# Attention, an MLP and eight experts in one kernel: the token scatters of the last batches spread out, and five slots' loads made independent of the last batch's scatters

## The chip, the cores and the metric

One core of a Trainium2 chip runs the whole program. The metric is device time in microseconds (us) of one execution; lower is better. The core has the engines that the profile calls PE (matrix multiplication), PEld (loading of its stationary operand), DVE (VectorE), ACT (ScalarE), POOL (GpSimd) and SP (SyncE, which here only issues transfers), and 16 DMA engines that all transfers share.

## The reference, cut to what matters

```python
scores = x @ state.T / sqrt(D); xread = softmax(scores) @ state      # 8 batches, 8 heads, 512 rows, D 64
sread  = softmax(state @ x.T / sqrt(D)) @ x                           # 32 rows of state for each batch
x = concatenate([xread, sread])                                       # 4096 + 512 rows -> 4608 tokens of 512
h = x @ w_in                                                          # 512 -> 2048
x = (h * clip(h + 3, 0, 6) / 6) @ w_out                               # 2048 -> 512
e_idx = argmax(x @ w_gate); gate_w = softmax(x @ w_gate)[e_idx]       # 8 experts, one for each token
eom = 1 / (1 + exp(-(x @ w_output_gate)))
for e in range(8):
    out[mask_e] = gate_w * eom[:, e] * (relu(x[mask_e] @ w1[e]) @ w2[e])   # 512 -> 1024 -> 512
```

## The kernel before

Tokens come in eight batches of 512 rows (the xread part, batches 0 to 7) and a last batch of 256 (the sread part). Each goes through attention and the MLP on PE, 16 steps of the hidden dimension ("ft") a batch; the sread steps are matmuls of line 473 into `h` and of lines 498 to 500 into `o`. While PE works on the next batch, the batch behind it is **routed**, in steps spread over the ft loop: its rows go out to memory (`xd`, line 543) and come back by token (`xt`, line 641), the expert is chosen, and VectorE works out each token's place (`place`, tile `ldsti`). Then POOL issues two kinds of indirect transfer, one for 128 tokens each: `sort_rows` (line 649) scatters rows of 2 KB into `xs`, which is sorted by expert, and `scatter` (line 663) scatters 8 bytes a token, its number and its weight, into the table `tab`. `zero_tails` (line 953) scatters four blocks of zeros into `xs`, from a tile that line 945 fills. Which of the two comes first on POOL is set by the program.

After the last batch, VectorE makes lists of the blocks to work on: `lists1` for blocks that surely hold tokens of batches 0 to 7 (kind "1"), `lists2` for those that depend on the last batch (kinds "m" and "p"). They land in `regs`, `regsm` and `regsu`, and SP reads addresses out of them (TENSOR_LOAD, lines 876 to 895; they can stand in front of SP's other work, and SP works strictly in its order).

The expert phase works through 16 slots of 256 rows, and in between pairs of two blocks of 64 rows. A slot is 8 ft steps: `gemm1` (12 matmuls of line 997, 128x256, into `h`) and `gemm2e` (6 matmuls of lines 1015, 1018 and 1019, 128x512, into `o`) with the pieces `wh`, `wl` (line 993), `vh`, `vl` (lines 1002, 1003), `hh` (line 1006) and `hl` (line 1007) that ACT and DVE make. At ft 3 of slot s, `turn` transposes the rows of slot s+1 on DVE (line 917) and rounds them (line 938), and `fetch_rows` has SP load the rows of slot s+3 (`xg`, line 897) with their token numbers and weights (`own`, line 906). At the end of a slot `fetch_weights` loads those of the slot after next (line 884, 8 transfers of 512 KB, left out at run time where the expert stays the same). `finish` scales the result by the weight (line 1032) and scatters it to `out` (line 1035). In `gemm1` this says that the low part of ft 6 comes behind the next rows on DVE:

```python
if ft == 6:
    tc.add_manual_dep(i.ins, last_turned[0].name, LATER, reason="the next rows first")
```

Every load of `xg` waits for the row scatters in the list `put`, every load of `own` for the token scatters in `placed`; each scatter waits for those of the batch before. The tiles for the rows, the zeros and the result `y` share a ring of two buffers ("xr"). Where nothing is stated, the order on an engine comes from a scheduler, not from the text alone.

Of the kernel before, what the change touches and what calls it, by code (L numbers as in the profile page):

```python
# [79 lines left out]
def tile_kernel(  # L80
# [421 lines left out]

    placed, put = [], []

# [139 lines left out]
    def sort_rows(r, t0, t1, behind=()):  # L644

        if t0 == 0:
            r.sorted = []
        for t in range(t0, t1):
            i = G.indirect_dma_start(xs, bass.IndirectOffsetOnAxis(ap=r.dsti[:, t:t + 1], axis=0), r.rows[t], None).ins  # L649
            for d in behind:  # L650
                tc.add_manual_dep(i, d.name, DEP, reason="in its time")
            for o in r.sorted:
                tc.declare_no_dep(i, o, reason="places are distinct")
            after(i, put)
            r.sorted.append(i)
        if t1 == r.nt:
            put[:] = r.sorted

    def scatter(r, behind=()):

        new = []
        for t in range(r.nt):
            i = G.indirect_dma_start(tab, bass.IndirectOffsetOnAxis(ap=r.dsti[:, t:t + 1], axis=0),
                                     toku[:, r.tile0 + t, :], None).ins
            for d in behind:
                tc.add_manual_dep(i, d.name, DEP, reason="rows are written first")
            tc.add_manual_dep(i, put[-1].name, LATER, reason="rows are wanted first")
            for o in new:
# [5 lines left out]
    def route(r):  # L674
# [15 lines left out]
        sort_rows(r, 0, r.nt)  # L690
        scatter(r)
        if r.n == 256:
            zero_tails()
        yield
# [192 lines left out]

    def load_rows(bases, n, own_by=None):
# [3 lines left out]
        own = cp.tile([128, 2, 2], U32, tag="own", name="own", bufs=5)  # L892
        a = n // 32
        for j, reg in enumerate(bases):
            base = D.value_load(reg, min_val=0, max_val=NTAB - n)
            for g in range(4):
                i = D.dma_start(xg[32 * g:32 * g + 32, a * j:a * j + a, :],
                                xs[bass.ds(base, n), 128 * g:128 * g + 128].rearrange("(a u) c -> u a c", u=32)).ins
                after(i, put)
            if n == 64:  # L900
                E = own_by or D
                if own_by:
                    base = E.value_load(reg, min_val=0, max_val=NTAB - n)
                i = E.dma_start(own[64 * j:64 * j + 64, 0, :], tab[bass.ds(base, n), :]).ins
# [3 lines left out]
        return own, xg  # L908

# [31 lines left out]

    def zero_tails():

        z = mp.tile([128, DM], F32, tag="xr", name="zeros", bufs=2)
        G.memset(z, 0.0)
        pair = carry.rearrange("p (j two) -> p two j", two=2)
        ends, tails = one("ends", NE // 2), one("tails", NE // 2, U32)
        V.tensor_tensor(ends, pair[:, 1, :], pair[:, 0, :], op=ALU.subtract)
        V.scalar_tensor_tensor(ends, ends, C("half"), pair[:, 0, :], op0=ALU.mult, op1=ALU.add)
        V.tensor_scalar(tails, ends, C("part64"), None, op0=ALU.add)  # L950
        new = []
        for j in range(NE // 2):
            i = G.indirect_dma_start(xs, bass.IndirectOffsetOnAxis(ap=tails[:, j:j + 1], axis=0), z, None).ins
            for o in new:
# [281 lines left out]

    got, turned, lists = {}, {}, {}

    def fetch_rows(s):
        k, j = ORDER[s]  # L1240
        regs = lists[k]
        n = regs.shape[1] // 3 * 2
        if k == "p":
            got[s] = load_rows([regs[0:1, n + u:n + u + 1] for u in (2 * j, 2 * j + 1)], 64, G if s >= first else None)
        else:
            got[s] = load_rows([regs[0:1, n + j:n + j + 1]], 256)

# [17 lines left out]
    for ft in range(16):  # L1265
        held.append((NB, ft, *act(h_sread(ft), 256, False)))
        second(LAG)
        step(later)
        step(later)
        if ft == 5:  # L1270
            while later:
                step(later)
            lists["1"] = lists1()
            fetch_weights(0)
            fetch_rows(0)

            for t in ws[1][0] + ws[1][1]:
                G.tensor_copy(t[0:1, 0, 0:1], got[0][1][0:1, 0, 0:1])
            fetch_weights(1)
# [5 lines left out]
    qa["p"].tile([128, 8], F32, name="gap2")  # L1285
    turned[0] = turn(got[0][1], 2)
    qa["p"].tile([128, 32], F32, name="gap3")
# [5 lines left out]
    def drain(n):  # L1293
        while len(pend) > n:
            s, py, args = pend.pop(0)
            gemm2e(py, *args)
            if args[0] == 7:
                ids, _ = got.pop(s)
                turned.pop(s)
                finish(py, ids, out[0:NX, :] if ORDER[s][0] == "1" else out, s + 1 == first)  # L1300

# [6 lines left out]
    def turn_next(s):  # L1308
        if s + 1 < first:
            turned[s + 1] = turn(got[s + 1][1], 1 if ORDER[s + 1][0] == 'p' else 2)  # L1310
        if s + 3 < first:
            fetch_rows(s + 3)

    def slot(s):
        g = big.index(s)
        for ft in range(8):
            if ft == 0 and s not in turned:
                turned[s] = turn(got[s][1], 1 if ORDER[s][0] == 'p' else 2)
            xh, xl = turned[s]
# [17 lines left out]
    def pair(s):  # L1337
        j = ORDER[s][1]
        if s not in turned:
            turned[s] = turn(got[s][1], 1 if ORDER[s][0] == 'p' else 2)  # L1340
        x, _ = turned.pop(s)
# [11 lines left out]
        for ft in range(8):  # L1353
# [4 lines left out]
            pair2(py, ft, hT[ft // 4])  # L1358
        finish([py], got.pop(s)[0], out)
        if j + 1 < NP and j + 1 != CUT:  # L1360
# [56 lines left out]
```

## Time and profile before

| | us |
|---|---|
| time, median of 3 runs | 1128.01 (1126.42 to 1130.27) |
| time of the profiled execution | 1126.77 |
| its span on the core | 1125.1 |
| PE busy in it | 1079.5 (96%) |
| DVE, ACT, POOL busy | 717.6, 553.3, 114.0 |

Times in the rows are counted from the start of the span. The span lies inside the execution's own time, and the two differ by 1.67 us here. Attention and the MLP of batches 0 to 7 end shortly after 630 us, the sread steps run to 693 us, the expert phase from 694 us to 1108.7 us.

### The profile page before, as it was taken

To read this page: it belongs to the slowest core of one execution; us is meant where nothing else is said; L and a number is where in the kernel's file an instruction comes from. 1 tells how busy PE (TensorE), PEld (TensorE's weight loads), DVE (VectorE), ACT (ScalarE), POOL (GpSimd) and SP (SyncE) were. 2 spreads that over 40 slices of the span, in tenths; PEclk is the share of its full clock that TensorE was granted. 3 is DMA by queue.
4 is the path that set the end of the run, shared out by engine and by line. 5 is a ranking of instruction groups with operands and counts; after the bars stand their busy time and mean duration, and the time that the engine had idled before them with its cause. 6 is when DMAs were issued, how large, how long until landed. Compare 5 with 4: busy or idle time off the path is not lost. (4 is left out here: it accounts for less than half of the span.)

```text
span 1125.1 us, 18656 instructions
## 1 busy us (share of the span) xinstructions
PE 1079.5 (96%) x6764; PEld 850.8 (76%) x6764; DVE 717.6 (64%) x1533; ACT 553.3 (49%) x1058; POOL 114.0 (10%) x122
## 2 busy tenths in 40 slices
PE   4899999999999999999999999999999999999994
PEld 2567777777777777777777889878869877889981
DVE  6997767755746747557455466886556756676640
ACT  4779744433434434334343435556445645665640
POOL 0000001120030020200300220310010110100010
PEclk9999999999999999999999999999999999999997
DMA  6647042622214114220130189267585689921300
GB/s 229 206 133 263 29 134 74 174 75 57 94 40 112 41 38 113 78 58 19 38 75 7 43 215 257 80 202 258 174 314 171 223 265 315 327 57 60 139 19 31
DMA packets 83428, 147.39 MB, mean 131 GB/s; under 512 B 13232, under 2 KB 49840, under 8 KB 83312
## 3 DMA queue, kind: packets, MB, share of 16 engines
q1 hardware_dynamic: 76400, 126.94, 36.8%
q0 software_dynamic: 6928, 19.18, 4.6%
q8 instruction: 55, 0.90, 0.3%
q14 instruction: 45, 0.37, 0.1%
HBM read 146.05 MB, written 29.68 MB: 156 GB/s over the span
## 5 line engine op out<-in xcount | busy, mean ns | idle before, releaser
L498 PE MATMUL o<-gh,wo 128*128 128x512 f32 x512 | 199.2, 393 | 1.7 <-ACT wo L752 1.7
L499 PE MATMUL o<-gh,wo 128*128 128x512 f32 x512 | 200.2, 391 | 0.6 <-DVE wo L753 0.6
L500 PE MATMUL o<-gl,wo 128*128 128x512 f32 x512 | 199.9, 390 | 0.0
L489 DVE SCALAR_TENSOR_TENSOR g<-r,h 128x512 f32<-128x512 f32 x128 | 87.4, 683 | 118.6 <-ACT r L488 118.0
L488 ACT ACTIVATE r<-h 128x512 f32<-128x512 f32 x128 | 76.7, 599 | 164.5 <-PE h L459 164.4
L1003 DVE TENSOR_TENSOR vl<-w2s,vh 128x512 fp32r<-128x512 f32 x128 | 87.7, 689 | 66.9 <-ACT vh L1002 62.9
L1002 ACT CAST vh<-w2s 128x512 fp32r<-128x512 f32 x128 | 78.8, 621 | 81.8 <-PE o L1019 73.5
L490 ACT CAST gh<-g 128x512 fp32r<-128x512 f32 x128 | 79.3, 620 | 80.2 <-DVE g L489 79.3
L491 DVE TENSOR_TENSOR gl<-g,gh 128x512 fp32r<-128x512 f32 x128 | 88.3, 690 | 45.5 <-ACT gh L490 37.9
L498 PEld LDWEIGHTS o<-gh,wo 128*128 128x128 f32 x512 | 95.9, 188 | 27.8 <-issue 4.4
L499 PEld LDWEIGHTS o<-gh,wo 128*128 128x128 f32 x512 | 96.3, 188 | 23.5 <-issue 2.1
L500 PEld LDWEIGHTS o<-gl,wo 128*128 128x128 f32 x512 | 96.1, 188 | 20.4
L993 DVE TENSOR_TENSOR wl<-w1s,wh 128x512 fp32r<-128x512 f32 x128 | 86.9, 687 | 37.3 <-ACT wh L993 29.5
L459 PE MATMUL h<-ah,sh 128*128 128x512 f32 x256 | 106.5, 417 | 4.0 <-ACT sh L446 2.3
L459 PE MATMUL h<-al,sh 128*128 128x512 f32 x256 | 102.3, 400 | 0.3 <-DVE al L290 0.3
L1019 PE MATMUL o<-vh,hl 128*128 128x512 f32 x256 | 100.7, 394 | 1.6 <-DVE hl L1007 1.6
L459 PE MATMUL h<-ah,sl 128*128 128x512 f32 x256 | 100.8, 394 | 0.0
L1018 PE MATMUL o<-vl,hh 128*128 128x512 f32 x256 | 100.3, 392 | 0.0
L649 POOL DMA_INDIRECT xs<-xt,ldsti x34 | 36.1, 1061 | 574.0 <-DVE ldsti L634 525.5
L993 ACT CAST wh<-w1s 128x512 fp32r<-128x512 f32 x128 | 77.9, 621 | 31.7 <-PE h L997 24.6
L997 PEld LDWEIGHTS h<-xh,wh 128*128 128x128 f32 x512 | 76.6, 188 | 15.0 <-DVE hl L1007 2.4
L997 PE MATMUL h<-xh,wh 128*128 128x256 f32 x512 | 82.3, 282 | 1.8 <-DVE hl L1007 1.8
(230 smaller groups left out, 1804.2 us busy)
## 6 DMA issues: line engine op xcount, KB each, us to landing
w1s<-w SPq DMA_DIRECT2D x88, 512.0 KB
w2s<-w SPq DMA_DIRECT2D x88, 512.0 KB
xd<-xr SPq DMA_DIRECT2D x68, 128.0 KB
xt<-xd SPq DMA_DIRECT2D x17, 512.0 KB
xT<-xT SPq DMA_DIRECT2D x16, 512.0 KB
wi<-w_in SPq DMA_DIRECT2D x16, 512.0 KB
wraw<-w_out SPq DMA_DIRECT2D x16, 512.0 KB
xq<-xq SPq DMA_DIRECT2D x16, 512.0 KB
```

The source lines that it names most:

```text
L459: T.matmul(ps, w[:, o:o + 128], a[:, e, :], start=(n == 0), stop=(n == 5))
L489: V.scalar_tensor_tensor(g6, r, 6.0, ps, op0=ALU.min, op1=ALU.mult)
L490: S.copy(gh, g6)
L491: V.tensor_tensor(gl, g6, gh.bitcast(F32), op=ALU.subtract)
L498: T.matmul(po[k][:, :n], woh[ft][:, s], gh, start=first, stop=False)
L499: T.matmul(po[k][:, :n], wol[ft][:, s], gh, start=False, stop=False)
L500: T.matmul(po[k][:, :n], woh[ft][:, s], gl, start=False, stop=last)
L993: last_w[:] = [S.copy(wh, a).ins, V.tensor_tensor(wl, a, wh.bitcast(F32), op=ALU.subtract).ins]
L997: T.matmul(ps, w[:, k, :], x[:, k, :], start=(m == 0), stop=(m == 11))
L1003: V.tensor_tensor(vl, c, vh.bitcast(F32), op=ALU.subtract)
L1018: T.matmul(py[t], hh[:, sl], vl, start=False, stop=False)
L1019: T.matmul(py[t], hl[:, sl], vh, start=False, stop=(ft == 7))
```

## The change

- The token scatter of batch 7 (4 transfers), so far right behind its row scatters, moves to ft 9 of the sread loop.
- The last batch's two token scatters come ahead of its row scatters on POOL, and its four scatters of zeros go out in two halves, some steps later. The memset of the zeros moves from POOL to VectorE.
- The last batch's row, token and zero scatters are declared independent of the loads of the slots of kind "1" (slots 0 to 4): those wait for batch 7's scatters only.
- `own` is loaded when the slot's rows are turned (`turn_rows`), no longer with the rows; the order for the `lists2` step at slot 1 no longer drains the routing steps first.

```diff
@@ -651,6 +659,8 @@
             for o in r.sorted:
                 tc.declare_no_dep(i, o, reason="places are distinct")
+            if r.n == 256:
+                apart(i, later_rows, sooner)
             after(i, put)
@@ -664,7 +674,8 @@
                 tc.add_manual_dep(i, d.name, DEP, reason="rows are written first")
-            tc.add_manual_dep(i, put[-1].name, LATER, reason="rows are wanted first")
+            if r.n == 256:
+                apart(i, later_rows, sooner)
@@ -688,9 +699,16 @@
         sort_rows(r, 0, r.nt)
-        scatter(r)
-        if r.n == 256:
-            zero_tails()
+        if r.n > 256:
+            return
+        yield
+        yield
+        scatter(r, last_w[:1])
+        yield
+        yield
+        zero_tails(0, 2)
+        yield
+        zero_tails(2, 4)
         yield
@@ -897,15 +914,23 @@
                 after(i, put)
+                if put is first_put:
+                    apart(i, sooner, later_rows)
+        return xg
...
+            if placed is first_placed:
+                apart(i, sooner, later_rows)
+        return own
@@ -939,18 +964,23 @@
-        G.memset(z, 0.0)
...
+            V.memset(zeros["z"], 0.0)
...
+        for j in range(j0, j1):
+            i = G.indirect_dma_start(xs, bass.IndirectOffsetOnAxis(ap=zeros["at"][:, j:j + 1], axis=0), zeros["z"], None).ins
+            tc.add_manual_dep(i, last_w[0].name, DEP, reason="in its time")
@@ -1265,17 +1300,23 @@
+        if ft == 9:
+            scatter(unplaced, marks[-1:])
+            first_placed[:] = placed
         if ft == 5:
             while later:
                 step(later)
+            first_put[:] = put
             lists["1"] = lists1()
@@ -1307,15 +1347,13 @@
     def turn_next(s):
         if s + 1 < first:
-            turned[s + 1] = turn(got[s + 1][1], 1 if ORDER[s + 1][0] == 'p' else 2)
+            turn_rows(s + 1)
@@ -1325,8 +1363,6 @@
             if s == 1 and ft == 0:
-                while later:
-                    step(later)
                 lists.update(lists2())
```

Where instructions stand now, at the places that the prediction speaks of:

On POOL, from batch 7's token scatters (`tab<-toku`) to the first results (`out<-y`); the 8 copies stand behind the loading of slot 0. Before:

```order
L663 DMA tab<-toku,ldsti 36096x2 x4
...
L945 MEMSET zeros 128x512
L649 DMA xs<-xt,ldsti 36096x512 x2
L663 DMA tab<-toku,ldsti 36096x2 x2
L953 DMA xs<-zeros,tails 36096x512 x4
L1035 DMA out<-y,own 4096x512 x10
```

Now:

```order
L673 DMA tab<-toku,ldsti 36096x2 x2
L657 DMA xs<-xt,ldsti 36096x512 x2
L981 DMA xs<-zeros,tails 36096x512 x2
L1065 DMA out<-y,own 4096x512 x2
L981 DMA xs<-zeros,tails 36096x512 x2
```

The memset is gone from POOL, the last batch's token scatters stand ahead of its row scatters, and slot 0's two result scatters stand between the two halves of the zeros. Batch 7's four token scatters keep their place in the row of POOL's work; what they wait for has changed.

On SP, from the last batch's rows to the weights of slot 2. Before, the rows and the `own` of slot 3 stand behind 25 reads of registers (TENSOR_LOAD), of which the last five are of lists that `lists2` makes:

```order
L641 DMA xt<-xd 128x2x512
...
L895 TENSOR_LOAD regsm
L895 ISA x2
L876 TENSOR_LOAD regsu
...
L895 TENSOR_LOAD regsu
L895 ISA x2
L897 ISA
L897 DMA xg<-xs 32x8x128
...
L906 DMA own<-tab 128x2x2
L884 ISA
L884 DMA w1s_5999<-w 128x1024
```

Now:

```order
L649 DMA xt<-xd 128x2x512
L914 ISA
L914 DMA xg<-xs 32x8x128
...
L894 TENSOR_LOAD regs_6345
L894 ISA x2
L897 TENSOR_LOAD regs_6345
L897 ISA x2
L902 ISA
L902 DMA w1s_5999<-w 128x1024
```

The reads of `regsm` and `regsu` have left this place, so that the rows of slot 3 and the weights of slot 2 stand in front of everything that waits for `lists2`.

On PE, from slot 1 into slot 2 (`o_7690` and `o_7691` before, `o_7713` and `o_7714` now, are slot 2's sums). Before:

```order
L997 MATMUL h<-xh,wh 128x256 x4
L997 MATMUL h<-xl,wh 128x256 x4
L997 MATMUL h<-xh,wl 128x256 x4
L997 MATMUL h<-xh,wh 128x256 x4
L997 MATMUL h<-xl,wh 128x256 x3
L1015 MATMUL o_7690<-vh,hh 128x512
L1015 MATMUL o_7691<-vh,hh 128x512
L997 MATMUL h<-xl,wh 128x256
L997 MATMUL h<-xh,wl 128x256 x3
```

Now:

```order
L1027 MATMUL h<-xh,wh 128x256 x4
L1027 MATMUL h<-xl,wh 128x256 x4
L1027 MATMUL h<-xh,wl 128x256 x4
L1045 MATMUL o_7713<-vh,hh 128x512
L1045 MATMUL o_7714<-vh,hh 128x512
L1048 MATMUL o_7713<-vl,hh 128x512
L1049 MATMUL o_7713<-vh,hl 128x512
L1048 MATMUL o_7714<-vl,hh 128x512
L1049 MATMUL o_7714<-vh,hl 128x512
```

Before, nearly four steps' first products (43 matmuls) stand ahead of slot 2's first second product; now the two kinds alternate step by step there. The bunched order stands before at the entries of slots 2, 3 and 11 with 43 matmuls, and of slot 7 with 55; now at those of slots 3, 7 and 11, with 43 each. The number of PE's instructions is the same.

## Rows read from the trace of the kernel before

**Rows 1.** The page, part 1: busy time of each engine.

```profile
PE 1079.5 (96%) x6764; PEld 850.8 (76%) x6764; DVE 717.6 (64%) x1533; ACT 553.3 (49%) x1058; POOL 114.0 (10%) x122
```

**Rows 2.** Waits of PE: what it waited for, us in total, times, longest.

```profile
PE h L473 <- issue: 2.4, 5, 0.9
```

**Rows 3.** Timeline of PE in the sread steps: start, us, instruction.

```profile
659.24 0.64 PE L473 MATMUL h<-x1h,wih 128*128 128x256 f32 x4
...
662.09 0.63 PE L473 MATMUL h<-x1h,wih 128*128 128x256 f32 x3
...
669.97 0.67 PE L473 MATMUL h<-x1h,wih 128*128 128x256 f32 x4
```

**Rows 4.** Windows: busy PE, PEld, DVE, ACT, POOL; granted clock, DMA share, GB/s.

```profile
665.00:670.00 5.00, 4.06 (x19) 3.70 (x19) 2.03 (x4) 2.11 (x5) 0.35 (x1) 0.66 0.98 211
670.00:675.00 5.00, 5.00 (x44) 5.00 (x44) 2.61 (x7) 2.62 (x6) 0.00 (x0) 0.99 0.98 255
735.00:740.00 5.00, 3.76 (x22) 2.83 (x20) 5.00 (x17) 2.30 (x5) 0.00 (x0) 1.00 0.17 58
```

**Rows 5.** Timeline of POOL: start, us, instruction, idle before it.

```profile
660.43 1.13 POOL L663 DMA_INDIRECT tab<-toku,ldsti  x1 [0.30 <-issue]
...
732.07 0.96 POOL L1035 DMA_INDIRECT out<-y,own  x1 [12.14 <-ACT y L1032]
```

**Rows 6.** DMA issues, 660:670, median us to landing.

```profile
tab<-toku,ldsti POOLq DMA_INDIRECT x4, 10.2
```

**Rows 7.** DMA issues, 620:640, median us to landing.

```profile
tab<-toku,ldsti POOLq DMA_INDIRECT x4, 3.7
```

**Rows 8.** Timeline of SP's queue: issues of weights, skipped ones too.

```profile
661.55 2.53 SPq L884 DMA_DIRECT2D w1s<-w  x4
...
741.69 1.39 SPq L884 DMA_DIRECT2D w1s<-w  x4
...
781.20 2.49 SPq L884 DMA_DIRECT2D w1s<-w  x4
```

**Rows 9.** Waits of SP's queue.

```profile
SPq L895 <- DVE regsm L803: 13.3, 1, 13.3
```

**Rows 10.** Timeline of DVE: the turn of slot 1's rows, and the end of slot 1.

```profile
710.25 1.42 DVE L917 STREAM_TRANSPOSE xt<-xg 128x256 f32<-128x256 f32 x4
...
739.91 0.75 DVE L1007 SCALAR_TENSOR_TENSOR hl<-h,hh 128x256 fp32r<-128x256 f32 x2
```

**Rows 11.** Timeline of ACT at the entry of slot 2.

```profile
741.79 0.62 ACT L993 CAST wh<-w1s 128x512 fp32r<-128x512 f32 x1 [2.40 <-DMA w1s<-w]
742.32 1.26 ACT L1032 ACTIVATE y<-o,own 128x512 f32<-128x512 f32 x2
```

**Rows 12.** Timeline of PE: end of slot 1, and a regular step of slot 2.

```profile
740.39 0.72 PE L1019 MATMUL o<-vh,hl 128*128 128x512 f32 x2 [1.63 <-DVE hl L1007]
...
753.75 0.63 PE L997 MATMUL h<-xh,wh 128*128 128x256 f32 x4
...
755.15 0.63 PE L1015 MATMUL o<-vh,hh 128*128 128x512 f32 x2
...
756.53 0.63 PE L997 MATMUL h<-xh,wh 128*128 128x256 f32 x4
```

**Rows 13.** Timeline of PE: entries of slots 3, 4 and 7.

```profile
766.25 0.63 PE L997 MATMUL h<-xh,wh 128*128 128x256 f32 x4
...
777.41 0.63 PE L997 MATMUL h<-xh,wh 128*128 128x256 f32 x4
...
793.40 0.74 PE L1015 MATMUL o<-vh,hh 128*128 128x512 f32 x2 [0.49 <-ACT hh L1006]
...
873.68 0.52 PE L997 MATMUL h<-xh,wh 128*128 128x256 f32 x3
...
886.74 0.63 PE L997 MATMUL h<-xh,wh 128*128 128x256 f32 x4
```

**Rows 14.** Tile trow, the other memset of this shape on DVE: ns, start.

```profile
L1069 DVE MEMSET trow<- x1: 485/485/485, 84.4 to 84.4; 128x512 f32 x1
```

More of the change, by code (lines that the diff above doesn't have):

```diff
@@ L500, in gemm2, with apart @@
             T.matmul(po[k][:, :n], woh[ft][:, s], gl, start=False, stop=last)
-    placed, put = [], []
+    placed, put, first_placed, first_put = [], [], [], []
+    sooner, later_rows = [], []
+    def apart(i, mine, others):
+        for o in others:
+            tc.declare_no_dep(i, o, reason="rows of earlier batches")
+        mine.append(i)
     def after(i, others):
@@ L886, in tile_kernel, with load_rows @@
     qa = {}
-    def load_rows(bases, n, own_by=None):
+    def load_rows(bases, n, put):
         xg = qa["p"].tile([128, 8, 128], F32, tag="xg", name="xg", bufs=2) if qa else \
             mp.tile([128, 8, 128], F32, tag="xr", name="xg0", bufs=2)
-        own = cp.tile([128, 2, 2], U32, tag="own", name="own", bufs=5)
         a = n // 32
@@ L899, in load_rows, with load_own @@
                 after(i, put)
+                if put is first_put:
+                    apart(i, sooner, later_rows)
+        return xg
+    def load_own(bases, n, placed):
+        own = cp.tile([128, 2, 2], U32, tag="own", name="own", bufs=5)
+        for j, reg in enumerate(bases):
+            base = D.value_load(reg, min_val=0, max_val=NTAB - n)
             if n == 64:
[L901 to L904, printed above, removed]
+                i = D.dma_start(own[64 * j:64 * j + 64, 0, :], tab[bass.ds(base, n), :]).ins
             else:
@@ L940, in turn, with zero_tails @@
         return xh, xl
-    def zero_tails():
-        z = mp.tile([128, DM], F32, tag="xr", name="zeros", bufs=2)
-        G.memset(z, 0.0)
[L946 to L950, printed above, removed]
+    zeros = {}
+    def zero_tails(j0, j1):
+        if j0 == 0:
+            zeros["z"] = mp.tile([128, DM], F32, tag="xr", name="zeros", bufs=2)
+            V.memset(zeros["z"], 0.0)
+            pair = carry.rearrange("p (j two) -> p two j", two=2)
+            ends, zeros["at"] = one("ends", NE // 2), one("tails", NE // 2, U32)
+            V.tensor_tensor(ends, pair[:, 1, :], pair[:, 0, :], op=ALU.subtract)
+            V.scalar_tensor_tensor(ends, ends, C("half"), pair[:, 0, :], op0=ALU.mult, op1=ALU.add)
+            V.tensor_scalar(zeros["at"], ends, C("part64"), None, op0=ALU.add)
         new = []
-        for j in range(NE // 2):
-            i = G.indirect_dma_start(xs, bass.IndirectOffsetOnAxis(ap=tails[:, j:j + 1], axis=0), z, None).ins
+        for j in range(j0, j1):
+            i = G.indirect_dma_start(xs, bass.IndirectOffsetOnAxis(ap=zeros["at"][:, j:j + 1], axis=0), zeros["z"], None).ins
+            tc.add_manual_dep(i, last_w[0].name, DEP, reason="in its time")
+            apart(i, later_rows, sooner)
             for o in new:
@@ L1242, in fetch_rows, with turn_rows @@
         n = regs.shape[1] // 3 * 2
[L1243 to L1246, printed above, removed]
+        at = (2 * j, 2 * j + 1) if k == "p" else (j,)
+        return [regs[0:1, n + u:n + u + 1] for u in at], 64 if k == "p" else 256
+    def fetch_rows(s):
+        got[s] = load_rows(*place_of(s), first_put if ORDER[s][0] == "1" else put)
+    def turn_rows(s):
+        turned[s] = turn(got.pop(s), 1 if ORDER[s][0] == 'p' else 2)
+        owns[s] = load_own(*place_of(s), first_placed if ORDER[s][0] == "1" else placed)
     big = [s for s, (k, _) in enumerate(ORDER) if k != "p"]
@@ L1267, in tile_kernel @@
         second(LAG)
+        if later and isinstance(later[0], Route):
+            unplaced = later[0]
         step(later)
         step(later)
+        if ft == 9:
+            scatter(unplaced, marks[-1:])
+            first_placed[:] = placed
         if ft == 5:
```

18 lines of the change are left out of this document (7 added, 11 removed).

## The prediction, made before the changed kernel had run

> **What bounds the kernel now.** I read the page first: PE is busy for 1079.5 of the 1125.1 us of the span [rows 1], so all that another engine does counts only where PE stands still for it, and 45.6 us is the most that any order of work could give back. Some 22 us of it are in the first 75 us and 16.4 us behind the last matmul (span 1125.1, last matmul at 1108.7); the change touches neither. Then I read the waits of PE and its timeline between 650 and 900 us, where the moved instructions stand. Three places show time lost.
>
> The first is a pause in the sread steps. Step 7 takes 662.09 − 659.24 = 2.85 us, and step 8 takes 669.97 − 662.09 = 7.88 us with the same matmuls [rows 3]: 5.0 us are lost. PE's waits put 2.4 us of it down to "issue", in 5 pieces [rows 2], that is to no semaphore which the profile shows; the rest is matmuls at a granted clock of 0.66 in the mean over 665 to 670 us [rows 4], part of it at the lower level of 1.2 GHz, after PE had stood still. Two things begin just then: POOL issues batch 7's four token scatters from 660.43 on [rows 5], and SP the 4 MB of slot 0's weights at 661.55 [rows 8]. The DMA engines are then 98% busy, and stay so from 670 to 675 us, when PE is busy for all 5.00 us [rows 4]. So full DMA engines alone do not stop PE; the token scatters among them, or the start of the loads, may.
>
> The second is the entry of slot 2. DVE is busy for all of 735 to 740 us, with `lists2` and the next rows, and PE waits 1.63 us for `hl` [rows 4, 12]. SP has meanwhile stood for 13.3 us before a register of `regsm` [rows 9], so that the (skipped) weight transfers of slot 2 come at 741.69 only [rows 8], and ACT's first piece of them after a wait of 2.40 us [rows 11].
>
> The third is small: the bunched order at the entries of some slots, and 0.49 us before slot 4 [rows 13].
>
> **The change, step by step.** All terms are in the profiled execution's time.
>
> *The memset on DVE.* The same shape took 485 ns on DVE [rows 14]. At its new place, among the `lists2` work, DVE has no gap before the `hl` that PE waits for at 740.39 [rows 10, 12]. It costs 0 if it falls before DVE fills up, and 0.5 if not. The order puts it in the middle of the filled stretch, so I take **+0.4**.
>
> *The bunched order at slot 2 goes.* A regular step is 12 first products, 755.15 − 753.75 = 1.40 us, and 6 second ones, 756.53 − 755.15 = 1.38 us [rows 12]. From 740.39 to 753.75 PE had 48 of the first and 26 of the second kind to do: 4 × 1.40 + 26 × 0.23 = 11.58 us of work. It took 13.36, so 1.78 us were lost behind the late weights and the bunching. Now SP has slot 2's weights in front of all that waits for `lists2`, and PE's order is regular there. The bounds are 0 (another wait is there) and −1.78. I take **−1.7**, because the wait of ACT that fed it, 2.40 us, ended on the weights alone.
>
> *The same at slot 7.* There the bunch shrinks from 55 to 43. The old one took 886.74 − 873.68 = 13.06 us for 60 and 24, which is 5 × 1.40 + 4 × 1.38 = 12.52 us of work: 0.54 lost. One of 43, at slot 3, took 777.41 − 766.25 = 11.16 us for 48 and 18, 9.74 us of work: 1.42 lost [rows 13]. The new bunch has the size of the second row, so I take 1.42 − 0.54 = **+0.9**; the bounds are 0 and +0.9. Slots 3 and 11 keep theirs.
>
> *SP runs earlier.* Slot 4's weights were issued at 781.20 [rows 8], late since SP was late from 741 on, and PE waited 0.49 for the `hh` made of them [rows 13]. SP gains several us before that, so this goes: **−0.5**, with bounds 0 and −0.5.
>
> *`own` with the turn.* Same number of transfers, one slot later. `own` is wanted only when the slot's result is scaled, a slot (8 × 2.78 = 22 us) after its turn; SP's load of it waits for batch 7's token scatters, which land by 672 + 4 × 1.3 + 10.2, about 687 us, before slot 0 begins at 694: 0.
>
> *The last batch's scatters.* Slot 3's first load now stands in front of the reading of the last batch's rows on SP. It waits for the buffer that the turn at 710.25 to 711.67 frees [rows 10]. So those rows are scattered some 8 us later, and the two halves of the zeros go out at about 728 and, behind slot 0's results on POOL (732.07 [rows 5] and one more), at 735 to 737. Landing takes 3.7 us where the DMA engines are quiet [rows 7], so the zeros' tile comes free at about 740. The second result tile takes its buffer, and ACT writes it at 742.32 [rows 11]. The cover is 2 us. It costs 0, and if it were gone, ACT would stand for as long as the zeros are late, with slot 2's pieces of weights behind it, and PE a step later.
>
> *Batch 7's token scatter to ft 9.* This is the large one. It waits for a mark of ft 9 now: about 672 us if the pause stays where it is, 667 if not. SP's loads of the weights of slots 0 and 1 (8 MB) run until about 700 us, so the scatter still falls into full DMA engines. The bounds: −5.0 (the pause needs the scatters and the start of the loads together, and the two are parted now), 0 (it moves with the scatters, or stays with the loads) and +5.0 (both make one). The row nearest to the scatter's new place is that of 10.2 us to land among loads, against 3.7 without [rows 6, 7]; the new place has the loads of the old one, which is why I take **0**. Against it stands that PE ran freely at 670 to 675 us while the same transfers were still landing [rows 4]: it is their issue that coincides with the pause, not their landing.
>
> The Trainium skill, page "DMA: Bandwidth & Descriptors", section "Issuing engines are not separate DMA queues", says that transfers started by the scalar, sync or GpSimd engine all run on the same 16 DMA engines and interleave. The trace agrees with it (10.2 against 3.7 us to landing). By it, moving the scatters by 7 to 12 us within the loads parts nothing, and the term is 0; by the row of 670 to 675 alone it would be −5.0.
>
> The sum is 0.4 − 1.7 + 0.9 − 0.5 + 0 = −0.9: 1126.77 − 0.9 = 1125.9 us. The profiled execution lies 1128.01 − 1126.77 = 1.24 us under the median of the runs, so I forecast 1125.9 + 1.24 = **1127.1 us**. About 0.3%, or 3.4 us, is what a measurement of this kernel can tell from no change.
>
> **The rivals.**
>
> *The pause goes.* The token scatters and the start of the weight loads no longer meet, and step 8 takes 2.85 us like its neighbours. For it: no such pause shows at 620 to 640 us, where four token scatters went out without loads, and none at 670 to 675 us, where loads ran without an issue of scatters. Against it: the scatters still go out among loads. 1127.1 − 5.0 = 1122.1 us.
>
> *A second pause.* The start of the loads, and the row scatter that POOL issued just ahead, make the pause at 662, and it stays; the token scatters, issued one by one into DMA engines that are 98% busy, make another at 672. The point that decides is whether PE's matmuls show "issue" at two places. For it: PE's order and SP's loads at 661 are the same as before, and at the new place the DMA engines are busy for 98% from the first scatter on [rows 4]. Against it: only one such case is in the trace. 1127.1 + 5.0 = 1132.1 us: slower.
>
> *The change does not do what it says.* Slot 3's load blocks SP as the register reads did, or the lists come no earlier, and slot 2 starts as before: the terms −1.7 and −0.5 go, and so would what follows from them. 1128 us.
>
> **How the numbers follow.** I give the forecast 0.50: its own range, from the bounds of its small terms (0 to 0.5, −1.8 to 0, 0 to 0.9, −0.5 to 0, together −2.3 to +1.4) and the spread of the runs, is 1124.5 to 1129.5. The pause that goes has 0.32, the second pause 0.12, the change that does nothing 0.06. Faster by over 0.3% means below 1124.6: the second case and the edge of the first, 0.37. Slower by over 0.3% means above 1131.4: the third and the edge, 0.13. Within it 0.50. To leave out no more than 2 in 10 the range must reach to the pause that goes, 1122.1 with some 1.5 us under it, so from 1120.5; above it goes to 1130.8, a little past the forecast's own, which leaves out most of the second pause.
>
> **What would show it.** In the changed kernel: PE's waits for "issue" in line 473 stay at about 2.4 us, at 662 or at 672; if they are gone, the first rival holds, and two groups of them are the second. Slot 2's entry shows no wait of ACT for weights and regular steps of 2.78 us; SP shows slot 2's weights well before 741 us. Slot 7's entry takes some 11.2 us for its 48 and 18. The wait for `hl` at the end of slot 1 is about 2.0 us. The prediction is wrong if PE waits at slot 1 for a result tile, or if a pause shows up that the trace before has nothing of.

## The result, and the profile after

The changed kernel takes 1115.81 us in the median of 4 runs (1115.35 to 1116.51), the kernel before 1128.33 beside it (1126.42 to 1130.27): a ratio of 0.989, 95% interval [0.9871, 0.9908]. It is 12.5 us faster, and the time lies under the forecast range. The profiled execution has a span of 1114.35 us, 10.78 less than that of before, and its own time is 1116.13; the rest of the 12.5 is that the profiled run of before lay 1.56 us under its median and this one 0.32 above.

Where those 10.78 us went, by the starts of the first product of each slot in PE's timeline:

| stretch | before | after | difference |
|---|---|---|---|
| start to slot 0 | 693.90 | 688.96 | −4.94 |
| slots 0 and 1 | 48.55 | 45.45 | −3.10 |
| slots 2 and 3 | 46.10 | 45.99 | −0.11 |
| slot 4 and its pair | 40.45 | 39.52 | −0.93 |
| slots 5 and 6 | 44.67 | 44.67 | 0 |
| slot 7 | 21.43 | 22.30 | +0.87 |
| slot 8 and its pair | 39.83 | 39.54 | −0.29 |
| slot 9 to the last matmul | 173.79 | 174.15 | +0.36 |
| last matmul to the end of the span | 16.38 | 13.76 | −2.62 |

First the sread steps, in PE's timeline (start, us, instruction):

```profile
662.20 0.64 PE L473 MATMUL h<-x1h,wih 128*128 128x256 f32 x4
...
665.05 0.64 PE L473 MATMUL h<-x1h,wih 128*128 128x256 f32 x4
```

Step 8 takes 665.05 − 662.20 = 2.85 us, where it took 7.88 [rows 3]. The windows there (busy PE, PEld, DVE, ACT, POOL; clock, DMA share, GB/s) show PE busy throughout at the full clock, with the DMA engines as full from 665 us on as before (1.01 against 0.98 [rows 4]):

```profile
660.00:665.00 5.00, 5.00 (x44) 5.00 (x44) 3.27 (x11) 2.51 (x6) 0.22 (x1) 1.00 0.69 249
665.00:670.00 5.00, 5.00 (x44) 5.00 (x44) 2.19 (x6) 2.61 (x6) 1.96 (x3) 1.00 1.01 322
```

POOL issues batch 7's token scatters after an idle time of 7.2 us behind its row scatters, among SP's loads, and PE does not stop. The timeline of POOL (the last line is the third scatter of zeros):

```profile
659.15 1.07 POOL L657 DMA_INDIRECT xs<-xt,ldsti  x1 [0.30 <-issue]
667.43 0.99 POOL L673 DMA_INDIRECT tab<-toku,ldsti  x1 [7.21 <-ACT rg L488]
...
729.91 0.96 POOL L981 DMA_INDIRECT xs<-zeros,tails  x1 [0.30 <-issue]
```

SP's issues of slot 0's, 2's and 4's weights:

```profile
661.24 2.04 SPq L902 DMA_DIRECT2D w1s<-w  x4
...
711.08 1.40 SPq L902 DMA_DIRECT2D w1s<-w  x4
...
769.95 2.48 SPq L902 DMA_DIRECT2D w1s<-w  x4
```

Slot 2's weights are dealt with at 711.08 instead of 741.69, slot 4's at 769.95 instead of 781.20 [rows 8]. The entries of slots 2 and 7 on PE's timeline:

```profile
733.84 0.73 PE L1049 MATMUL o<-vh,hl 128*128 128x512 f32 x2 [0.61 <-DVE hl L1037]
734.41 0.64 PE L1027 MATMUL h<-xh,wh 128*128 128x256 f32 x4
...
745.57 0.63 PE L1027 MATMUL h<-xh,wh 128*128 128x256 f32 x4
...
864.60 0.63 PE L1027 MATMUL h<-xh,wh 128*128 128x256 f32 x4
...
875.75 0.52 PE L1027 MATMUL h<-xh,wh 128*128 128x256 f32 x3
```

The tile of the zeros, ns and start of its memset:

```profile
L973 DVE MEMSET zeros<- x1: 485/485/485, 720.3 to 720.3; 128x512 f32 x1
```

PE waits 0.61 us for `hl` where it waited 1.63 [rows 12]. From the end of that wait, 48 first and 26 second products take 745.57 − 733.84 = 11.73 us, where the same number took 13.36, and the 48 and 18 products at slot 7's entry take 875.75 − 864.60 = 11.15 us.

The end is read from POOL. The views leave out semaphore instructions, but the trace has them. POOL's records from the last result scatter on (start, us, instruction; short ones are left out), before:

```
1109.78 0.96 DMA_INDIRECT out<-y,own
1110.58 0.02 EVENT_SEMAPHORE
1110.84 2.17 EVENT_SEMAPHORE
1113.13 2.32 INC_SWDGE_SEM
1115.48 8.80 DRAIN
```

and after:

```
1101.62 0.95 DMA_INDIRECT out<-y,own
1102.13 0.02 EVENT_SEMAPHORE
1102.28 0.04 EVENT_SEMAPHORE
1102.37 2.33 INC_SWDGE_SEM
1104.72 8.80 DRAIN
```

The semaphore instruction that took 2.17 us takes 0.04. What it waited for was the landing of the last result scatter: the semaphore of that transfer had its last update at 1112.97 us, and the instruction ended at 1113.01. In the changed kernel this landing, at 1104.35, falls within INC_SWDGE_SEM, and POOL does not wait for it ahead of that.

### The profile page after: what moved, and what is told of

Same layout as the page of the kernel before. It is cut to its first block, busy times and chain, and to the rows that moved or that the text cites. A ratio compares the mean times of both kernels' runs of the same rounds, so it can differ in the third digit from the quotient of the medians.

```text
span 1114.3 us, 18721 instructions
## 1 busy us (share of the span) xinstructions
PE 1075.0 (96%) x6764; PEld 848.7 (76%) x6764; DVE 718.3 (64%) x1534; ACT 552.9 (50%) x1058; POOL 113.0 (10%) x121
```

## The experiments

The groups ran on different chips, and this mattered: beside groups 1, 4 and 5 the kernel before took 1128.9, 1130.2 and 1129.1 us, beside groups 2 and 3 only 1118.5 and 1119.1. Times are therefore compared within a group. A group is one chip at one time, so that what is put down to the chip below may also be a matter of the occasion. Cuts in the edits are marked with `...`.

### Group 1: the scatter's place, the loads' place, and the part on the last batch

**scatter_back**, the changed kernel with batch 7's token scatters where they were:

```diff
+                tc.add_manual_dep(i, put[-1].name, LATER, reason="rows are wanted first")
...
         if r.n > 256:
+            scatter(r)
...
             return
...
-        if ft == 9:
-            scatter(unplaced, marks[-1:])
...
```

> The changed kernel with one edit: batch 7's four token scatters go out right behind its row scatters again, at about 660 us. Theory A (the scatters, issued while SP starts slot 0's weights, make the pause): PE's wait for issue in line 473 is back with some 2.4 us, step 8 of the sread steps takes about 7.9 us instead of 2.8, and the time is 5 us above the changed kernel's, about 1121. Rival B (the pause hung on something else that the change shifted, such as the length or the place of the instruction streams): no pause, about 1116.

1121.05 us. The pause is back: 6.0 us by the times against scatter_at_13 on the same chip. Its windows:

```profile
660.00:665.00 5.00, 3.20 (x22) 2.83 (x21) 0.19 (x2) 0.00 (x0) 3.81 (x4) 0.95 0.99 207
665.00:670.00 5.00, 4.53 (x21) 4.08 (x21) 2.48 (x5) 2.29 (x6) 0.00 (x0) 0.50 0.70 166
```

So this one move of four instructions takes the pause away, 5.9 us of the sread steps (60.99 against 55.13). Slot 1 took 23.18 us here, as in the changed kernel.

**weights_later**, the kernel before with the loading of slot 0 written three steps later:

```diff
         if ft == 5:
             lists["1"] = lists1()
+        if ft == 8:
             fetch_weights(0)
```

> The kernel before with one edit: the loading of slot 0's weights and rows starts three sread steps later, at about 669 us instead of 661.5, the token scatters stay at 660 to 665. Theory A (scatters and the start of the weight loads must meet): no pause at 662, step 8 takes about 2.8 us; a late weight may cost some of the 5 us at slot 0. Rival C (the four token scatters directly behind four row scatters are enough, whatever SP does): the pause of 5 us stays at 662. A third outcome, a pause at 669 with the loads, would put it on the loads alone.

1129.27 us, and nothing learnt on the theories: the order came out as before, SP began the loads at 662.94, and the pause was there. Code written later is not an instruction issued later. As a second profile of the old order it shows something else: slot 1 took 29.87 us here, against 26.29, with a wait of PE that the other does not have. It falls into the last batch's scatters, which before the change also went out eight in a row (from 709.85 to 719.8 us here):

```profile
721.67 0.56 PE L1015 MATMUL o<-vh,hh 128*128 128x512 f32 x1 [3.42 <-ACT hh L1006]
```

**scatter_at_13**:

```diff
-        if ft == 9:
+        if ft == 13:
             scatter(unplaced, marks[-1:])
```

> The changed kernel with one edit: batch 7's token scatters wait for step 13 instead of step 9 of the sread loop, so that they are issued at about 679 to 685 us, when SP starts the second 4 MB of weights (679.1 in the changed kernel). Theory A (scatters and the start of a weight load meet): a new pause of PE of about 5 us at 680, in lines 473 to 500, with waits for issue; about 1121. Rival C (it takes the row scatters just ahead as well): no pause, about 1116.

1115.01 us, no pause: scatters at 678.1 to 683 and SP's second 4 MB from 676.2 on meet, and PE is busy for all of it:

```profile
675.00:680.00 5.00, 5.00 (x44) 5.00 (x43) 2.68 (x6) 1.73 (x5) 2.76 (x10) 1.00 0.75 183
680.00:685.00 5.00, 5.00 (x44) 5.00 (x43) 2.48 (x7) 1.76 (x5) 2.35 (x3) 1.00 1.02 322
```

Theory A, in the form "token scatters and the start of a weight load", fell here.

**no_apart**: routing of the last batch as before, no `declare_no_dep` for it.

```diff
-            tc.declare_no_dep(i, o, reason="rows of earlier batches")
...
-        yield
-        yield
-        scatter(r, last_w[:1])
-        yield
-        yield
-        zero_tails(0, 2)
-        yield
-        zero_tails(2, 4)
+        scatter(r)
+        zero_tails(0, 4)
...
```

> The changed kernel without the part on the last batch: its rows, token numbers and zeros go out in one go as before, the loads of slots 0 to 4 wait for them again, and the routing steps are drained at slot 1. What stays: batch 7's token scatter at step 9, own loaded with the turn, the conditional pairs' own on SP, the memset on VectorE. Theory: the pause stays away (5 us), the end of the program is 2.6 us shorter than in the kernel before, and the 3.2 us at slots 0 to 2 and the 0.9 at slot 4 come back: about 1120. Rival: the gain at slots 0 to 2 comes from own being loaded with the turn, and not from the scatters being apart: about 1116.

1118.2 us, 3.2 above scatter_at_13; in the profiles slot 1 takes 25.27 instead of 23.24, and the rest of the difference lies ahead of the sread steps (they begin at 634.59 against 633.17, which varies from 631.2 to 635.5 over all runs). The wait for `hl` at the end of slot 1 is 1.3 us:

```profile
PE o L1038 <- DVE hl L1026: 1.3, 1, 1.3
```

The part on the last batch is worth 2.0 us at slot 1; why the sread steps begin later is not shown. The bunched order of 43 first products at slot 2's entry is back with it. The scatters of zeros came some 12 us behind the token scatters here, so that the old row of eight is not. Slot 4 kept its 39.52 us, so its gain is not of this part; the expectation had it among what comes back.

### Group 2: on a chip without the pause, as it turned out

**weights_wait**, scatter_back with a semaphore for slot 0's loads:

```diff
+                for o in held_back:
+                    tc.add_manual_dep(x.ins, o.name, DEP, reason="in its time")   # x: each weight load
...
+        if ft == 9:
+            held_back[:] = marks[-1:]
             fetch_weights(0)
...
```

> The kernel of scatter_back (batch 7's token scatters right behind its row scatters, with the pause) with one edit: slot 0's weights and rows are loaded only after a mark of step 9, about 667 us, so that SP starts no load while the scatters are issued at 659 to 665. Theory A2 (row scatters, token scatters and the start of the weight loads together make the pause): no pause in step 8, the DMA engines are free at 660 to 667; slots 0 and 1 may wait for weights. Rival C (eight scatters in a row are enough, without any load): the pause of 5 us stays in step 8, with 2 us of issue in line 473.

**tokens_first**:

```diff
         place(r)
+        if r.n > 256:
+            scatter(r)
...
+            sort_rows(r, 0, r.nt)
+            return
         sort_rows(r, 0, r.nt)
...
-        if ft == 9:
-            scatter(unplaced, marks[-1:])
...
```

> The changed kernel with one edit: batch 7's token scatters go out right ahead of its row scatters (about 655 to 660), the row scatters behind them (660 to 665), so that it is row scatters that are issued while SP starts the loads at 661. Theory A2 (eight scatters in a row meet the loads, whichever kind comes last): the pause is back, 1121. Rival D (it takes the small 8-byte pieces among the loads): no pause, about 1116, or a little more since slot 0's rows come 5 us later.

1119.99 and 1115.12 us, neither with a pause; but the kernel before beside them took 1118.46, 10 us less than on the chips seen so far, so that neither told anything on it. In weights_wait, slots 1 and 2 took 25.86 and 24.94 us with late weights.

**in_turn**, PE's order made regular:

```diff
+                if m == 0 and seconds:
+                    tc.add_manual_dep(i.ins, seconds[-1].name, LATER, reason="in turn")
...
+        seconds.append(i.ins)          # i: the last matmul of gemm2e
```

> The changed kernel with one edit: on PE, gemm1 of step f+2 has to stand behind gemm2e of step f, so that the bunched order (43 first products ahead of a slot's first second product) at the entries of slots 3, 7 and 11 becomes a regular one; nothing else is asked of any engine. Theory (the bunching itself costs what the working of the prediction took from the rows, 1.4 us each): three times 1.4 us less, about 1111.6. Rival (what the bunch waits for is there anyway, the weights or the low parts being late at a slot's entry): the waits move to the second products and the time stays within 1 us of the changed kernel's.

1127.97 us, 12.9 above tokens_first. Both theories were wrong. ScalarE kept its order (three `wh` in a row and a fourth ahead of the first `vh`), PE waited for `vh` and then `vl`, and ran at the lower clock after it; slots 3, 7 and 11 took 26.59, 27.57 and 26.41 us instead of 22.3. PE's waits in in_turn:

```profile
PE o L1049 <- ACT vh L1036: 7.3, 3, 2.4
...
PE o L1052 <- DVE vl L1037: 2.4, 3, 0.9
```

And a window at slot 3's entry, with the clock at 0.69:

```profile
765.00:770.00 5.00, 5.00 (x23) 4.46 (x23) 2.29 (x4) 1.62 (x4) 0.00 (x0) 0.69 0.14 41
```

**own_on_pool**:

```diff
-                i = D.dma_start(own[64 * j:64 * j + 64, 0, :], tab[bass.ds(base, n), :]).ins
+                E = own_by or D      # G for the conditional pairs
...
+                i = E.dma_start(own[64 * j:64 * j + 64, 0, :], tab[bass.ds(base, n), :]).ins
```

> The changed kernel with one edit: the own loads of the conditional pairs, which are not executed here, stand on POOL's queue again instead of SP's. Theory: the end of the program, from PE's last matmul to the end of the span, is 16.4 us again instead of 13.8, since POOL waits for the last result scatter before it clears its queue; nothing else changes, 1118.4. Rival: the end got shorter by something else (the order of the last scatters), it stays at 13.8 us and 1116.

1117.49 us, 2.4 above tokens_first. From the last matmul to the end it takes 16.34 us instead of 13.76, and POOL's record of 2.12 us is there again. Those loads never run here: that POOL would issue them in the branches not taken is enough.

### Group 3: the control

**before_again** is the kernel before; **scatter_back_2** and **weights_wait_2** are the kernels above.

> The kernel before, unchanged, profiled again as a control. In the runs beside weights_wait, tokens_first, in_turn and own_on_pool it took 1118.5 us instead of 1128. If the pause in step 8 belongs to the kernel on every chip, its profile shows 5 us there again. If it depends on the chip, a time of about 1118 goes with a profile without the pause.

> The kernel of scatter_back again, beside the control: 5 us above the changed kernel's and the pause in step 8 where the control shows it; 1116 and no pause where the control shows none.

> The kernel of weights_wait again, beside the control, since its first run had none with the pause: token scatters right behind the row scatters, slot 0's loads held back to step 9. Where the control shows the pause, Theory A2 (it takes the start of the weight loads) has none here; Rival C (eight scatters in a row are enough) has it here as well, 5 us in step 8.

1118.4, 1115.11 and 1120.09 us; the kernel before beside them 1119.13. No pause in any. In before_again the scatters start at 654.89 and 660.14 and SP's loads at 660.86, as on the other chips, and PE works through:

```profile
660.00:665.00 5.00, 5.00 (x44) 5.00 (x43) 3.00 (x8) 2.51 (x6) 3.94 (x4) 1.00 0.79 248
665.00:670.00 5.00, 5.00 (x45) 5.00 (x44) 2.52 (x6) 2.32 (x6) 0.17 (x1) 1.00 0.84 181
```

So the same program has the pause on one chip and not on another. Without it slot 1 of the kernel before took 24.64 us instead of 26.29 and slot 4 39.79 instead of 40.45: in these two profiles some 2.3 us behind the pause go with it. At slot 1 it is the wait for `hl`, of 0.27 us here against 1.63, and small stops ahead of it. The loss at slot 2's entry is there without the pause too: 48 first and 26 second products take 746.76 − 733.09 = 13.67 us.

```profile
733.09 0.73 PE L1019 MATMUL o<-vh,hl 128*128 128x512 f32 x2 [0.27 <-DVE hl L1007]
...
746.76 0.63 PE L997 MATMUL h<-xh,wh 128*128 128x256 f32 x4
```
Against scatter_back_2, which has all of the change but the scatter's place, the ratio is 0.9965 [0.9954, 0.9977]: 4.0 us.

**act_in_turn**, ScalarE's order made regular, and PE's with it:

```diff
+        if vhs:
+            tc.add_manual_dep(i, vhs[-1].name, LATER, reason="in turn")   # i: the cast to wh
...
+        vhs.append(S.copy(vh, c).ins)
```

> The changed kernel with one edit: on ScalarE, the first piece of a step's weights (wh) has to stand behind the second piece of the step before (vh). ScalarE's order and with it PE's are regular at the entries of slots 3, 7 and 11. In in_turn PE was made to go in turn while ScalarE still made three wh ahead of the first vh, and PE waited 2.4 us for vh three times and ran at the lower clock after it. Theory (the bunch is an order that the scheduler chose and no data is late there): three times 1.4 us less than the changed kernel. Rival (the weights of the second product land late): waits for vh stay, by DMA, and the time is that of the changed kernel or above.

1117.87 us, 2.8 above scatter_back_2. The bunches are gone, but PE waits 0.98 us for `vh` at the same three entries, behind ScalarE's two results of the slot before, and slots 0 and 1 take 1.2 and 0.9 us longer. The bunch is no loss that an order on one engine gives back.

```profile
760.65 0.73 PE L1050 MATMUL o<-vh,hh 128*128 128x512 f32 x2 [0.98 <-ACT vh L1037]
```

### Group 4: a chip with the pause

> The kernel of weights_wait once more: token scatters right behind the row scatters, slot 0's loads held back to step 9. If the kernel before takes 1128 beside it (a chip with the pause): Theory A2 (it takes the start of the weight loads) no pause in step 8, Rival C (eight scatters in a row are enough) 5 us there. If the kernel before takes 1118: nothing on this, 1120 as in the two runs so far.

> The kernel of tokens_first once more: batch 7's token scatters ahead of its row scatters, so that row scatters are issued while SP starts the loads. On a chip with the pause: Theory A2 (eight scatters in a row meet the loads, whichever kind is last) 1121 with the pause, Rival D (it takes the small pieces of 8 bytes among the loads) 1116 without it. On a chip without it: 1115.

**two_back** adds to scatter_back that only two of the four token scatters go out at once:

```diff
+            scatter(r, (), 0, 2)
...
         if ft == 9:
-            scatter(unplaced, marks[-1:])
+            scatter(unplaced, marks[-1:], 2)
```

> The changed kernel with one edit: two of batch 7's four token scatters go out right behind its row scatters, the other two at step 9. On a chip with the pause: about half of it (2 to 3 us in step 8) if it grows with the number of small pieces that meet the loads; all or nothing if it is a matter of a meeting at one moment. On a chip without it: 1115 to 1116.

> The changed kernel, unchanged, on this chip. On a chip with the pause 1116 against 1128. On a chip without it about 1115 against 1118.5: the gain is then only what is left without the pause, 2.6 us at the end of the program and the rest at slots 0 to 4, about 3.5 us or 0.3%.

1126.68, 1122.62, 1119.11 and 1116.76 us; the kernel before beside them 1130.15. The sread steps, 55.1 us where nothing stops (56.5 in the two runs of weights_wait without the pause), took 61.70, 61.42, 57.40 and 55.10. In weights_wait_3 SP starts no load before 672.63, and PE stops all the same. Its waits:

```profile
PE h L473 <- issue: 2.6, 5, 1.1
```

Its windows, with the DMA engines 21% and 1% busy:

```profile
660.00:665.00 5.00, 3.60 (x28) 3.18 (x26) 1.08 (x8) 0.41 (x1) 3.78 (x5) 1.00 0.21 76
665.00:670.00 5.00, 3.80 (x18) 3.31 (x18) 1.64 (x4) 2.06 (x5) 0.65 (x1) 0.73 0.01 0
```

And POOL's sixth to eighth scatter in its timeline:

```profile
662.17 0.96 POOL L673 DMA_INDIRECT tab<-toku,ldsti  x1 [0.30 <-issue]
663.43 0.96 POOL L673 DMA_INDIRECT tab<-toku,ldsti  x1 [0.30 <-issue]
664.70 0.95 POOL L673 DMA_INDIRECT tab<-toku,ldsti  x1 [0.30 <-issue]
```

Neither the loads nor a kind of scatter is needed, each taken by itself: weights_wait_3 stops without loads, tokens_first_2 with the row scatters in the last place. Without loads and with the rows last nothing was run. In all three PE first stops 0.8 to 0.9 us after POOL began the sixth scatter of its row (662.17 and 663.08 here), as in scatter_back; in weights_later it was 1.5 us. two_back, with six in a row, has two short stops, and its step 8 takes 4.32 us, 1.5 more than a regular one. PE's waits in it:

```profile
PE h L473 <- issue: 0.9, 2, 0.4
```

### Group 5: how unbroken a row

**short_break** has `if ft == 7` for the scatter; **unbroken** makes the scatters of batches 1 to 6 go out eight in a row:

```diff
-        at(11, lambda: place(r), lambda: sort_rows(r, 0, 2))
-        at(12, lambda: sort_rows(r, 2, 4, marks[-1:]))
-        at(13, lambda: scatter(r, marks[-1:]))
+        at(11, lambda: place(r))
+        at(13, lambda: sort_rows(r, 0, 4, marks[-1:]), lambda: scatter(r, marks[-1:]))
```

> The changed kernel with one edit: batch 7's token scatters wait for the mark of step 7 instead of step 9, about 1.5 us behind its row scatters instead of 0.3 (unbroken) or 7.2 (changed). On a chip with the pause (the kernel before takes 1128 to 1130 beside it): if the unbroken row is what counts, no pause, about 1116; if it is the number of scatters in some 10 us, most of the pause, 1119 to 1121. On a chip without it: about 1115.

> The changed kernel with one edit: in the six batches 1 to 6, whose scatters go out as two, two and four with breaks of 0.83 and 1.42 us, all eight wait for the mark of step 13 and go out in one row. Batch 7 stays apart. On a chip with the pause: if an unbroken row of eight makes it wherever it stands, six pauses of about 5 us with waits for issue in the lines of the xread steps, 1140 to 1146; if it takes the short 128x256 matmuls of the sread steps (an instruction each 0.12 us instead of 0.23), no pause and about 1116. On a chip without it: about 1115.

1117.51 and 1117.92 us, the kernel before 1129.05. The scheduler mixed rows and tokens in short_break, so that it has no break but an unbroken row of eight from 661.66 to 672.2, six microseconds later than before; PE stops there twice, late in that row (PE's timeline):

```profile
671.73 0.50 PE L473 MATMUL h<-x1l,wih 128*128 128x256 f32 x2 [0.16 <-issue]
672.06 0.68 PE L473 MATMUL h<-x1h,wil 128*128 128x256 f32 x3
673.18 0.38 PE L473 MATMUL h<-x1h,wil 128*128 128x256 f32 x1 [0.44 <-issue]
```

The sread steps took 56.61 us, 1.5 more than in the changed kernel. So eight in a row cost PE no more here than six in two_back. In unbroken the six rows of eight make no wait for issue at all: in the xread steps an unbroken row is not enough to stop PE.

## Why the prediction was wrong, step by step

*What bounds the kernel.* Right: all that was won is time in which PE stood still or ran at the lower clock. Wrong was "the change touches neither" as far as it says that of the end. The end got 2.62 us shorter, a quarter of the gain, as loads that never run left POOL's queue (own_on_pool). The prediction costed `own` by its transfers and its turn only, and passed over a part of the change: in the kernel before, the `own` of the conditional pairs was issued by POOL (`own_by` in `load_rows`), and now it is by SP.

*Batch 7's token scatter to ft 9.* This is the step that failed: "The row nearest to the scatter's new place is that of 10.2 us to land among loads ... which is why I take 0". It measured −4.94: with the issue of four transfers moved 8 us behind, step 8 takes 2.85 us, and scatter_back, which moves them back, loses 5.9 us in the sread steps. The value was taken from a row on landing, while the row that spoke on PE itself, full DMA engines with PE busy for 5.00 us [rows 4], pointed to the issue, as the prediction wrote beside it. The rival that the pause goes had 0.32 and its time of 1122.1 was still too high by 6.3, because of the end (2.6), of slots 0 to 4 (2.3) and of the step from the profiled run to the median (1.6). The rule of the Trainium skill ("DMA: Bandwidth & Descriptors", "Issuing engines are not separate DMA queues") gave 0 as well; it speaks of transfers, and weights_wait_3 shows that the pause does not need the transfers of the loads. The second pause did not come.

*The bunched order at slot 2 and the memset.* The first was right, in mechanism and size: −1.7 forecast, and the prediction's own stretch, from the end of the wait for `hl` through 48 first and 26 second products, went from 13.36 to 11.73 us, −1.63. The control, which has the old order and no pause, loses as much there as before, and in no_apart the bunch is back. The second was wrong: the memset took the 485 ns that it was given, but at 720.3, 13 us ahead of the `hl` that it was to delay, and the wait for `hl` fell by 1.0 instead of growing by 0.4. The remaining 0.6 of the 3.2 us at slots 0 to 3 are small stops of PE ahead of that wait, for which the prediction has no term. In the control the wait is 0.27 us and the small stops are not there either, and weights_later lost 3.6 us more at slot 1 than before: on a chip with the pause this loss varies from run to run. With the last batch's scatters spread out, slot 1 took 23.2 us in each of the eleven profiles that have its weights in time and the old order of ScalarE and PE, with the pause and without.

*Slot 7.* Forecast +0.9, measured +0.87, and 11.15 us for the 48 and 18 against "some 11.2". But in_turn and act_in_turn show that the 1.4 us are no price of the order as such: with a regular order about as much, or more, is lost there.

*SP runs earlier.* Forecast −0.5, measured −0.93. The wait at slot 4 is gone; in the control, without the pause, 0.66 of it was gone already.

*`own` with the turn, the last batch's scatters.* 0 at their places, as forecast: PE waits for no result tile at slot 1, and the zeros' last scatter starts at 731.17.

*The sum.* −0.9 forecast, −10.8 measured: 4.9 for the pause, 2.6 at the end, 1.9 more at slots 0 to 3 than forecast, 0.4 at slot 4, and small ones. Adding 1.24 us for the median erred in the same direction: the changed kernel's profiled run lay above its median. The gain is one of chips with the pause: on one without it the kernel that has all but the scatter's move is 4.0 us faster (group 3), 0.35%. The changed kernel itself was run on no such chip.

**What stays open.** Why PE stops is not settled. Shown: in the sread steps unbroken rows of six and eight indirect transfers on POOL make it stop and rows of four do not; it needs neither the loads nor a kind of scatter; it is there on some chips, or occasions, and not on others. A wait of PE for "issue" is not where it begins, though. ScalarE, which makes a `wih` for PE every 2.85 us, stood still before PE did, for the result `h` of products that PE has on record as done. Its waits, in before, in two_back, in the changed kernel, and in the control for comparison:

```profile
666.75 0.62 ACT L467 CAST wih<-win 128x512 fp32r<-128x512 f32 x1 [6.55 <-PE h L473]
...
665.33 0.62 ACT L467 CAST wih<-win 128x512 fp32r<-128x512 f32 x1 [3.84 <-remote]
...
673.20 0.62 ACT L467 CAST wih<-win 128x512 fp32r<-128x512 f32 x1 [1.98 <-PE h L473]
...
665.85 0.62 ACT L467 CAST wih<-win 128x512 fp32r<-128x512 f32 x1 [0.74 <-PE h L473]
```

In the five profiles that stop behind eight in a row at batch 7 this wait is 6.5 to 6.6 us, behind six 3.8, behind the four token scatters of the changed kernel still 2.0, which costs PE nothing; in the eight profiles of the chips without the pause it is never over 1.0 from 644 us on. So what a row on POOL holds up is word of PE's finished products, and the longer the row, the longer. In scatter_back PE's semaphore updates for four groups of products, done by the record at 658.8, 659.7, 660.2 and 661.6 us, come at 664.5 and, the other three, between 666.0 and 666.2. Whether the products or only the updates were late, the trace does not tell.

It does not take the short matmuls of line 473: in weights_later ScalarE stood for 4.36 us at slot 1, during the last batch's row of eight, for an update that is due at 716.9 by PE's record and came at 720.48; hence PE's wait of 3.42 us there. Why the rows of unbroken do no harm is open.

One more difference goes with the chips. Where there is no pause, the traces hold 8066 to 8079 semaphore updates by transfers, elsewhere 7384 to 7517, the changed kernel's among them, with the same number of transfers: there, records were lost. All times here are of recorded runs, so whether the recording takes part in the pause is not tested. A late fetch of instructions does not show: the 16 KB taken to be PE's came at 658.44 and took 1.27 us in scatter_back, and at 658.49 and 1.16 us in scatter_at_13, which has no pause; the longest without a pause took 2.72 us (tokens_first). The Trainium skill ("Runtime: NRT & Kernel Launch", "Instruction fetch mechanics") has such fetches as mostly hidden, and these agree.

## What to carry to other kernels

A wait of PE for "issue", with a lower clock behind it, is lost time that no semaphore explains: look at what another engine issues in that moment and at which engines stand still for PE's results, and give the parting of the two a chance by the rows on issue, not by those on landing. Loads in branches that are not taken still cost at the end of the program, on the queue that would have issued them. Before a pause is explained, run the unchanged kernel on another chip: three groups of runs had this one and two had not. And before a term is called wrong, measure the stretch that it was worked out for: −1.7 was right, inside a sum that was not.

## What was not expected of the hardware

The same program took 1118.4 us on one chip and 1128 to 1130 on others, in runs of the same kind. Between the two profiled spans, 1125.1 and 1117.5 us, 5.1 of the 7.7 us are PE's pause in one place and 2.3 what was lost behind it, at slots 1 and 4. Eight indirect transfers in a row on POOL cost PE 5.2 us in weights_wait_3 (61.70 − 56.5) while the DMA engines were 21% and then 1% busy, six cost 1.5 in two_back, and eight at a later place 1.5 in short_break; ScalarE's wait for PE's results grew with the row, 2.0, 3.8 and 6.5 us behind four, six and eight, on these chips alone. Waits of PE of 2.4 us for `vh` and 0.8 for `vl`, at three entries of in_turn, made these slots 4.1 to 5.3 us longer than in the changed kernel, as the clock fell to 0.69 in the mean of the next 5 us. Transfers that POOL would issue in branches not taken made the end of the program 2.6 us longer (16.34 us in own_on_pool against 13.76).
